# One step of the preparation reordered in a fused attention and MLP kernel, and one small sum moved to another PSUM bank

## The chip, the cores and the metric

The kernel runs on one core of a Trainium2 chip. A core has a matrix engine (TensorE, PE in the profile, with its weight loads as PEld), a vector engine (VectorE, DVE), a scalar engine (ScalarE, ACT), a general engine (GpSimd, POOL) and SyncE (SP), which issues most DMAs here. The metric is the device time of one execution in microseconds, as the median over several runs. Lower is better.

## What is computed

The input x has 2048 tokens of 640 numbers. A layer normalization gives xn, and two blocks read it side by side:

```
xn  = layernorm(x)
A   = attention(xn @ wqkv) @ wo        # 32 heads of 20, softmax over 2048 keys
B   = gelu(layernorm(xn) @ w1 + b1) @ w2 + b2    # 640 -> 1536 -> 640, per token
out = x + A + B
```

All inputs are float32. The kernel splits most numbers into a high and a low 16-bit part and multiplies in three passes (high x high, high x low, low x high), so that a product costs three matmuls.

## The kernel before

The kernel has two stages. The first is a preparation, about the first 183 us. It normalizes the tokens, turns them so that the feature axis lies on the partitions, and projects them to queries, keys and values. The second stage is a long loop over 16 pairs of heads, where the attention's scores and products alternate with pieces of the MLP. The change lies in the preparation alone.

**Chunks and steps.** The preparation takes the tokens in four chunks (c = 0 to 3) of 512. For each chunk it makes five products (tt = 0 to 4) of 30 matmuls, `qk(c, tt)` at L352, each giving 256 rows of the queries and keys. Right after a product is issued, a string of letters says which other work is issued then, letter by letter. Instructions run on each engine in the order in which they are issued, and SyncE's queue takes its DMAs in that order too. Nothing is reordered later by a planner: a manual schedule is in force, and waits are set by data alone. So the string is the order of work on every engine at once.

**The letters that the change touches** are those of chunk 0, product 4:

- `4`: `lengths(4)`, the squared lengths of four blocks, 16 small matmuls on TensorE (L397).
- `!`, `@`, `#`: `transp`, the transposes of the next chunk (chunk 1) on TensorE (L314), two feature blocks each for the first two and one for the third. `!` and `@` write to score buffers in PSUM, `#` to the one-bank pool `psM`.
- `t`: `transp_out`, which takes the oldest turned tile out of PSUM: ScalarE writes the high part (L321), VectorE the low part (L322). The third `t` also issues the store of the whole turned chunk to memory, `xscr`, on SyncE (L324). The main loop reads it much later.
- `o`: `qk_out`, which takes the product just made out of PSUM (ScalarE L367, VectorE L368) and issues two stores, `qkscr` (L373).
- `c`: `norm_c`, the last three small operations (L249 to L251) for the rows' factors `rall` of chunk 1. They are read at the end of the preparation.
- `q`: a load of one row block of w1, 768 KB (L545). `y`: a load of two row blocks of w2, 640 KB (L539). `x`: `load_x(2)`, four loads of chunk 2's tokens, 320 KB each (L197). All on SyncE.
- `S`: squares of the product's result on ScalarE (L384). `w`: the scale of the value weights (`scale_of`, L118 and L119 on) and their split (L476, L477). `z`: the next slice of the second layer's scale, a sum of squares over the rows of w2 that the latest `y` loads brought, on ScalarE (L530).

**Around it.** Chunk 1, product 0 issues `zos`: ScalarE squares the rows of w2 from the second `y` (L530), then `qk_out`, then a slice of w1's squares (L507). Chunk 1, product 1 issues, among others, `a` (`norm_a(2)`: the statistics of chunk 2's tokens on VectorE, L263 and L264), `b` (`norm_b(2)`, L278) and `i`, which with `j`, `k`, `l` is `turn`: ScalarE and VectorE split a tile into high and low parts (L333, L334), and SyncE issues a turning DMA (L335). Chunks 2 and 3 are turned by those DMAs, chunk 1 by TensorE.

**PSUM.** `psS` has three score buffers of two banks, `psO` one bank and `psM` one bank. A product, a transposed pair and most scale sums take the next free buffer of `psS`. `pow2(acc, tag)` at L109 to L126 turns sums of squares into a power of two: two matmuls with ones (L118) add over the partitions, and VectorE reduces and rounds (L119 on). The tag tells which weights: q, k, v, o, 1, 2 or b1. The first layer's scale, tag 1, is asked for in chunk 1, product 4, just ahead of chunk 2's first product. `psM` is what the MLP's products use in the main loop; in the preparation it also holds key lengths and the third transposed block.

Of the kernel before, what the change touches and what calls it, by code (L numbers as in the profile page):

```python
# [48 lines left out]
def mha_mlp_kernel(tc, x, wqkv, wo, w1, b1, w2, b2, out):  # L49
# [4 lines left out]
    with (  # L54
# [53 lines left out]
        def pow2(acc, tag, total=None):  # L108

            lo = keep.tile([P, 1], F32, name=f"lo_{tag}")  # L110
            hi = keep.tile([P, 1], F32, name=f"hi_{tag}")
            if total is None:
                if tag in "ko":
                    pt = psM.tile([P, 512], F32, tag="m", name="mxp")
                else:
                    pt = psS.tile([P, 2, 512], F32, tag="s", name="mxp")[:, 0, :]
                n = acc.shape[1]
                nc.tensor.matmul(pt[:, :n], ones_of[0], acc, start=True, stop=True)  # L118
                nc.vector.tensor_reduce(lo, pt[:, :n], AX.X, ALU.add)  # L119
                total = lo  # L120
            nc.vector.tensor_scalar(lo, total, 2.0**-100, 2.0**120, ALU.max, ALU.min)

            nc.vector.tensor_scalar(lo.bitcast(I32), lo.bitcast(I32), 0x7F000000, 1,
                                    ALU.bitwise_and, ALU.logical_shift_right)
            if tag == "q":

                scales[tag] = keep.tile([P, 1], F32, name=f"s_{tag}")
                nc.vector.tensor_scalar(hi.bitcast(I32), lo.bitcast(I32), 0x3F800000, None, ALU.bitwise_xor)
                nc.vector.tensor_scalar(scales[tag], hi, 2.0**76, None, ALU.mult)
                return lo, hi  # L130
            whole(lo, hi)
            return lo, hi

        def whole(lo, hi):
            nc.vector.tensor_scalar(lo, lo, 2.0**64, None, ALU.mult)
            exponents(lo, hi)
# [42 lines left out]
        with tc.tile_pool(name="pa", bufs=2) as pa, tc.tile_pool(name="pa1", bufs=1) as pa1, tc.manual_schedule():  # L179
# [103 lines left out]
            def norm_b2(c):  # L283
                mv, ve, r, r2 = rs[c]

                nc.vector.tensor_mul(ve, r, r)
                nc.vector.scalar_tensor_tensor(ve, ve, 2.0**-20, mv[:, :, 1], ALU.mult, ALU.mult)
                nc.vector.tensor_scalar(ve, ve, EPS, None, ALU.add)
                nc.gpsimd.tensor_tensor(r2, ve, nhalf, ALU.pow)

            def norm_c(c):
                mv, ve, r, r2 = rs.pop(c)
                newton(r2, ve, "b")
# [49 lines left out]
            def qk(c, tt, mid=None):  # L343
                ps = psS.tile([P, 2, 512], F32, tag="s", name="qkp")
                order = [(i, k) for i in range(2) for k in range(KD)]
                if c == 0 and tt < 2:

                    order = [(i, k) for k in range(KD) for i in range(2)]
                for i, k in order:
                    q, mm = divmod(2 * tt + i, KD)  # L350
                    for n, (a, b) in enumerate(PASS):
                        nc.tensor.matmul(ps[:, i, :], wv[:, k, q, a, mm * P : (mm + 1) * P],  # L352
                                         xnts[c][:, k, b, :], start=(k + n == 0), stop=(k == KD - 1 and n == 2))
                    if mid and (i, k) == (1, 2):
                        mid()
                return ps
# [98 lines left out]
            def sums(tag, ws):  # L455
                accs[tag] = squares(ws, junk)

            def scale_of(tag, total=None):
                pw[tag] = pow2(accs[tag], tag, total)
                if tag not in scales:  # L460
                    scales[tag] = keep.tile([P, 1], F32, name=f"s_{tag}")
                    nc.vector.tensor_scalar(scales[tag], pw[tag][1], 4096.0, None, ALU.mult)
                if tag == "k":
                    back(tag)
# [8 lines left out]
            def split_qkv(n, ks=range(KD), c0=0, c1=D):  # L473
                q = "qkv".index(n)
                for k in ks:
                    nc.scalar.activation(wv[:, k, q, 0, c0:c1], stage[n][:, k, c0:c1], AF.Copy, scale=scales[n])  # L476
                    nc.vector.scalar_tensor_tensor(wv[:, k, q, 1, c0:c1], stage[n][:, k, c0:c1], scales[n],  # L477
                                                   wv[:, k, q, 0, c0:c1], ALU.mult, ALU.subtract)
# [72 lines left out]
            def ask(n):  # L551
                for _ in range(n):
                    next(asked, None)
# [3 lines left out]
            def some(n):  # L557
                for _ in range(n):
                    next(slices, None)
# [60 lines left out]
            for c in range(4):  # L620
                nxt = c + 1 if c < 3 else None
                for tt in range(5):
                    if c == 0 and tt == 1:
                        norm_b2(0)
                        norm_c(0)

                        nc.scalar.activation(junk[:, :1], ones[:, :1], AF.Exp)
                        ps = qk(0, 1, lambda: scale_of("k"))
                        hl = qk_out(0, 0, first)
                        split_qkv("q", c0=4 * P)  # L630
                        split_qkv("k")
                    else:
                        ps = qk(c, tt)
                    if c == 0:
                        if tt == 0:
                            split_qkv("q", c0=2 * P, c1=4 * P)
                            sums("k", [stage["k"][:, 0:3], stage["k"][:, 3:]])
                            first = ps
                            continue
                        elif tt == 1:  # L640
                            qk_sq(0, 0, hl)
                            pts = []
                    for step in (('', 'qvo', 'ao', 'bo', '4q!y@c#otyxttSywz'), ('zos', 'qa6yqoPsbiqs', 'jkso', 'lcsV4o', 'sxoy'), ('ssoa6bzijP', 'yo', 'zs4ossc', 'klozV', 'uozs'), ('so', 'os6', 'oszs', 'ssosPsVfze4', 'o'))[c][tt]:
                        if step == "a":
                            norm_a(nxt)
                        elif step == "b":
                            norm_b(nxt)
                        elif step == "c":
                            norm_c(nxt)
                        elif step in "!@#":  # L650
                            transp(1, 2 * "!@#".index(step), pts)
                        elif step == "t":
                            transp_out(*pts.pop(0))
                        elif step in "46":
                            lengths(int(step))
                        elif step == "x":
                            load_x(c + 2)
                        elif step == "s":
                            some(1)
                        elif step == "q":  # L660
                            ask(1)
                        elif step == "z":
                            next(slices2, None)
                        elif step == "y":
                            next(asked2, None)
                        elif step == "v":
                            sums("v", [stage["v"][:, 0:3], stage["v"][:, 3:]])
                        elif step == "w":
                            scale_of("v")
                            split_qkv("v")  # L670
                        elif step == "u":
                            for s in range(2):
                                nc.sync.dma_start(vwscr[:, :, s], wv[:, :, 2, s, VC:])
                        elif step == "f":
                            factors_out()
                        elif step == "S":
                            qk_sq(0, 4, hl)
                        elif step == "o":
                            hl = qk_out(c, tt, ps)
                        elif step == "P":  # L680
                            vp = vproj(c - 1)
                        elif step == "V":
                            head_values(c - 1, vp)
                        elif step == "e":
                            early = [load_features(mc) for mc in range(2)]
                        else:
                            turn(nxt, "ijkl".index(step))
# [789 lines left out]
```

## Time and profile before

| | us |
|---|---|
| median of 3 runs | 1329.0 (1326.13 to 1329.7) |
| the profiled execution | 1328.16 |
| its span, first to last instruction | 1326.3 |
| TensorE busy | 1314.0 |
| ScalarE busy | 1116.3 |
| VectorE busy | 1065.3 |

The profile is of one execution. Its span is what the instructions cover, and the execution's own time is a little longer. A busy share is an average over the whole span: TensorE's 99% hides a few short waits in the preparation, and what a change there is worth is read from the order of time around it, from who waits for whom. An engine's idle time before an instruction stands in square brackets, with the one that ended it. That name is inferred from the semaphores: where an instruction waits for several, it is the one that came last by the profile, and it can be wrong. DMAs are seen as issues on SyncE's queue (their length is the time in the queue, not the transfer), as bytes moved per time, and through the waits that they end.

### The profile page before, as it was taken

What the parts mean: (1) busy time and instruction counts of PE and PEld (TensorE: products, weight loads), DVE (VectorE), ACT (ScalarE), POOL (GpSimd) and SP (SyncE); (2) the same over time, 40 slices, a digit from 0 to 9 for tenths busy, and PEclk for the clock granted to TensorE, in tenths of its full rate; (3) what the DMA queues carried; (4) which work ended last, traced back from release to release, by engine and by line L of the source; (5) the groups of instructions that cost most, each with busy time, mean ns of one, the idle gap of its engine ahead of it and who ended that gap; (6) DMA issues with size and microseconds to landing.
All of it is one profiled execution on the core that took longest, in us unless ns stands there. A gap on an engine that the chain in (4) does not pass through costs nothing.

```text
span 1326.3 us, 29078 instructions
## 1 busy us (share of the span) xinstructions
PE 1314.0 (99%) x11636; PEld 604.2 (46%) x11636; DVE 1065.3 (80%) x1450; ACT 1116.3 (84%) x1306; POOL 36.1 (3%) x85
## 2 busy tenths in 40 slices
PE   9999999999999999999999999999999999999998
PEld 6454564333344444444444444444444444443466
DVE  7667569898699887889988798987889898988642
ACT  7745369999999999999999999999999999989900
POOL 2000000000000000000000000000000000000000
PEclk9999999999999999999999999999999999999999
DMA  8697531121233321142312034222124332253266
GB/s 308 215 276 214 190 103 35 39 63 53 77 82 99 86 57 33 44 120 64 97 47 68 17 88 123 69 55 58 50 59 117 92 87 70 71 158 100 87 216 192
DMA packets 108166, 135.28 MB, mean 102 GB/s; under 512 B 24308, under 2 KB 74376, under 8 KB 107900
## 3 DMA queue, kind: packets, MB, share of 16 engines
q1 hardware_dynamic: 104588, 125.99, 31.9%
q0 software_dynamic: 2816, 6.90, 2.7%
q8 instruction: 92, 1.51, 0.5%
q10 hardware_dynamic: 624, 0.51, 0.1%
q14 instruction: 46, 0.38, 0.1%
HBM read 86.64 MB, written 43.74 MB: 98 GB/s over the span
## 4 chain that ended last, share of the span: by engine, by line
PE 72%; DVE 15%; ACT 5%; DMA 4%; issue 2%; SPq 1%; ACTq 0%; DVEq 0%; POOLq 0%
PE o L818 23%; PE s L786 15%; PE pu L1079 10%; PE py L1114 8%; DVE low L800 6%; PE qkp L352 6%; PE z L1264 5%; PE pz L1166 3%; ACT p L788 2%; PE vp L425 1%; DMA xb<-in_B_b_dram 1%; DVE w L1014 1%; DVE u L1012 1%; DVE u L1010 1%; DVE w L1016 1%
## 5 line engine op out<-in xcount | busy, mean ns | idle before, releaser
L788 ACT ACTIVATE p<-s 128x1024 f32<-128x1024 f32 x1024 | 968.7, 1057 | 56.2 <-PE s L786 53.9
L800 DVE TENSOR_TENSOR low<-p 128x1024 f16<-128x1024 f32 x512 | 605.7, 1219 | 72.8 <-ACT p L788 71.4
L818 PE MATMUL o<-p,vfull 128*32 128x512 bf16 (+1 forms) x4096 | 384.1, 493 | 0.0
L786 PE MATMUL s<-qs,ks 61*128 61x512 f16 x2048 | 303.5, 381 | 3.0 <-ACT p L788 2.1
L786 PEld LDWEIGHTS <-ks 61*128 61x128 f16 x2048 | 75.7, 94 | 234.8 <-issue 215.8
L1114 PE MATMUL py<-w2t,hT 128*128 128x320 f16 x1152 | 171.5, 300 | 0.9 <-DVE xb L1041 0.9
L1079 PE MATMUL pu<-xm,w1t 128*128 128x256 f16 x1440 | 171.4, 273 | 0.1
L1079 PEld LDWEIGHTS <-w1t 128*128 128x128 f16 x1440 | 134.3, 98 | 43.9 <-issue 29.3
L818 PEld LDWEIGHTS <-vfull 128*32 128x32 f16 x3072 | 61.1, 95 | 183.3 <-issue 182.7
L1114 PEld LDWEIGHTS <-hT 128*128 128x128 f16 x1152 | 105.6, 98 | 71.2 <-issue 33.9
L352 PE MATMUL qkp<-xnt,wv 128*128 128x512 f16 x600 | 131.4, 379 | 1.6 <-DVE lo L119 0.8
L818 PE MATMUL o<-low,vfull 128*32 128x512 f16 x1024 | 101.5, 378 | 0.1
L352 PEld LDWEIGHTS <-wv 128*128 128x128 f16 x600 | 58.0, 98 | 70.9 <-issue 1.7
L818 PEld LDWEIGHTS o<-p,vfull 128*32 128x32 f32 x2048 | 61.8, 108 | 58.3
L1264 PE MATMUL z<-w1t,ot 128*128 128x320 f16 x480 | 66.7, 299 | 0.0
L1010 DVE TENSOR_TENSOR u<-pu,r2f 128x512 f32<-128x512 f32 x48 | 33.1, 689 | 36.2 <-PE pu L1079 36.0
L1264 PEld LDWEIGHTS <-ot 128*128 128x128 f16 x480 | 46.3, 98 | 21.0 <-issue 3.3
L367 ACT ACTIVATE qkhl<-qkp,qks 128x1024 f16<-128x1024 f32 (+1 forms) x24 | 23.2, 965 | 37.2 <-PE qkp L352 15.3
L1221 DVE SCALAR_TENSOR_TENSOR acc<-z,sc,acc 128x320 f32<-128x320 f32 x32 | 17.6, 550 | 42.0 <-PE z L1264 41.7
L368 DVE SCALAR_TENSOR_TENSOR qkhl<-qkp,qks,qkhl 128x1024 f16<-128x1024 f32 (+1 forms) x24 | 26.5, 1105 | 26.1 <-ACT qkhl L367 26.0
L843 ACT ACTIVATE ev<-o 128x512 f32<-128x512 f32 x64 | 39.5, 617 | 3.0 <-PE o L818 2.8
L1104 POOL DMA_DIRECT2D xb<-in_B_b_dram x16 | 13.7, 857 | 953.7 <-DMA xb<-in_A_x_dram 352.4
(206 smaller groups left out, 735.2 us busy)
## 6 DMA issues: line engine op xcount, KB each, us to landing
qkscr<-qkhl SPq DMA_DIRECT2D x40, 256.0 KB
opart<-ev SPq DMA_DIRECT2D x124, 80.0 KB
ks<-qkscr SPq DMA_DIRECT2D x120, 80.0 KB
xm<-xscr SPq DMA_DIRECT2D x13, 640.0 KB
qs<-qkscr SPq DMA_DIRECT2D x192, 40.0 KB
oa<-opart SPq DMA_DIRECT2D x32, 240.0 KB
xt<-in_A_x_dram SPq DMA_DIRECT2D x16, 320.0 KB
xscr<-xnt SPq DMA_DIRECT2D x4, 1280.0 KB
```

Source lines behind the costliest of these rows:

```text
L352: nc.tensor.matmul(ps[:, i, :], wv[:, k, q, a, mm * P : (mm + 1) * P], xnts[c][:, k, b, :], start=(k + n == 0), stop=(k == KD - 1 and n == 2))
L368: nc.vector.scalar_tensor_tensor(hl[:, 1, i0:i1], ps[:, i0:i1], a, hl[:, 0, i0:i1], ALU.mult, ALU.subtract)
L786: nc.tensor.matmul(ps[:, a, :], ks[64 * a : 64 * a + 61, kb * P : (kb + 1) * P], qs[64 * a : 64 * a + 61, cc * 512 : (cc + 1) * 512], star ...
L788: nc.scalar.activation(pt, ps, AF.Exp, scale=QS)
L800: nc.vector.tensor_sub(low, pt, upper(pt))
L818: nc.tensor.matmul(pv.o[32 * q : 32 * q + 32, :], src[:, v0 - PAD * (1 - q % 2) :][:, :32], t, start=q not in pv.begun, stop=last, skip_gr ...
L843: nc.scalar.activation(evs[g, hf][:, cc], o, AF.Copy)
L1010: nc.vector.tensor_mul(u, ps, r2f[:, None, :].to_broadcast([P, 2, MC]))
L1079: nc.tensor.matmul(ps[:, i], w1v[:, k, (f + i) // 4, a, fo_ : fo_ + P], xnt[:, k, b, :], start=(n == 0), stop=(n == 3 * KD - 1))
L1114: nc.tensor.matmul(ps[:, :320], hTs[mc][:, f, a, j * P : (j + 1) * P], w2v[:, f, b, hf * 320 : (hf + 1) * 320], start=(n == 0), stop=(n == ...
L1166: nc.tensor.matmul(ps[:, : D - VC], feats[c][:, k, a, j * P : (j + 1) * P], hv[:, k, b, :], start=(n == 0), stop=(n == 3 * KD - 1))
L1264: nc.tensor.matmul(ps[:, :320], ot[:, k, a, j * P : (j + 1) * P], wov[:, k, b, h * 320 : (h + 1) * 320], start=(n == 0), stop=(n == 3 * KD ...
```

## The change

It has two parts. In the string of chunk 0, product 4 the three transposes now come ahead of the lengths, the factors `c` come after two turned tiles in place of before the third transpose, and with that the DMAs change places: the w1 load comes after the first w2 load, and the third turned tile, with its store, comes ahead of the second w2 load and of the four token loads. The set of letters is the same, and no other step's string differs. In `pow2`, tag 1 joins k and o: its sum is made in `psM` in place of a score buffer.

```diff
             if total is None:
-                if tag in "ko":
+                if tag in "ko1":
                     pt = psM.tile([P, 512], F32, tag="m", name="mxp")
                 else:
                     pt = psS.tile([P, 2, 512], F32, tag="s", name="mxp")[:, 0, :]
...
-                    for step in (('', 'qvo', 'ao', 'bo', '4q!y@c#otyxttSywz'), ('zos', 'qa6yqoPsbiqs', 'jkso', 'lcsV4o', 'sxoy'), ...
-                    for step in (('', 'qvo', 'ao', 'bo', '4q!y@c#otyxttSywz'), ('zos', 'qa6yqoPsbiqs', 'jkso', 'lcsV4o', 'sxoy'), ('ssoa6bzijP', 'yo', 'zs4ossc', 'klozV', 'uozs'), ('so', 'os6', 'oszs', 'ssosPsVfze4', 'o'))[c][tt]:
+                    for step in (('', 'qvo', 'ao', 'bo', '!y@#4qottctyxSywz'), ('zos', 'qa6yqoPsbiqs', 'jkso', 'lcsV4o', 'sxoy'), ('ssoa6bzijP', 'yo', 'zs4ossc', 'klozV', 'uozs'), ('so', 'os6', 'oszs', 'ssosPsVfze4', 'o'))[c][tt]:
```

## The prediction

> **What bounds the kernel now.** I read the page first, then the chain that ended last, in order of time, then the stretch from 47 to 92 us instruction by instruction, and last SyncE's issues with the bytes that the DMAs moved.
>
> ```profile
> span 1326.3 us, 29078 instructions
> PE 1314.0 (99%) x11636; PEld 604.2 (46%) x11636; DVE 1065.3 (80%) x1450; ACT 1116.3 (84%) x1306; POOL 36.1 (3%) x85
> PE 72%; DVE 15%; ACT 5%; DMA 4%; issue 2%; SPq 1%; ACTq 0%; DVEq 0%; POOLq 0%
> ```
>
> Over the whole span TensorE is the bound. The reordered step lies near 50 us, so the chain around it decides (start, length, what):
>
> ```profile
> 49.07 0.17 DVE bt L250
> ...
> 49.38 1.28 DVE qkhl L368
> 50.67 1.14 DVE xnt L322
> ...
> 51.85 13.11 PE qkp L352 x60
> 64.96 0.26 PE norms L397 x8
> ...
> 65.25 0.69 DVE sq L386
> 65.94 0.81 DVE st L263 x2
> ...
> 75.50 0.74 DVE row L334
> ...
> 76.28 2.53 SPq L335
> ```
>
> Up to 51.85 us VectorE sets the pace, then TensorE until 64.96. Then VectorE normalizes the third chunk (65.25 to 76.24, back to back), and from 76.28 SyncE issues the DMAs that turn it. TensorE meets that chunk at 90.48:
>
> ```profile
> SPq L338 <- DMA xnt<-row: 2.7, 1, 2.7
> 90.45 1.64 PEld L352 LDWEIGHTS <-wv 128*128 128x128 f16 x9 [0.89 <-issue]
> 90.46 0.56 SPq L338 DMA_DIRECT2D xscr<-xnt  x1
> 90.48 1.89 PE L352 MATMUL qkp<-xnt,wv 128*128 128x512 f16 x8 [0.83 <-DVE lo L119]
> 90.48:182.80 92.32, 92.31 (x649) 51.10 (x649) 56.85 (x134) 37.02 (x63) 5.91 (x9) 1.00 0.66 193
> ```
>
> The matmul's wait of 0.83 us is put down to the reduction at L119. But the weight load ahead of it started at 90.45, and SyncE's store at 90.46 ended a wait for the turned chunk itself, so I read all three as released by the last turning DMA. The last row (a window, TensorE's busy time first) shows TensorE without a gap from there to 182.80. So whatever moves the third chunk's turning moves everything behind it.
>
> **The change part by part.**
>
> *Transposes ahead of the lengths, factors later (TensorE and VectorE).*
>
> ```profile
> 47.43 0.41 PE L397 MATMUL norms<-sq,heads 128*32 128x128 bf16 x16
> 47.68 1.28 DVE L368 SCALAR_TENSOR_TENSOR qkhl<-qkp,qks,qkhl 128x1024 f16<-128x1024 f32 x1
> 49.02 1.53 PE L314 MATMUL pt<-ident,xt 128*128 128x128 f32 x12 [0.16 <-DVE qkhl L368]
> 50.59 2.94 DVE L322 TENSOR_TENSOR xnt<-pt,xnt 128x1024 f16<-128x1024 f32 x3
> 50.73 0.38 PE L118 MATMUL mxp<-acc,ones 128*128 128x2 f32 x2 [0.17 <-DVE qkhl L368]
> 51.85 13.11 PE L352 MATMUL qkp<-xnt,wv 128*128 128x512 f16 x60 [0.75 <-DVE xnt L322]
> ```
>
> The three small factor operations (L249 to L251) stand between the two L368 and hold the second one from 47.68 + 1.28 = 48.96, when the first has ended, to 49.38. Moved behind two turned tiles they let it start 0.4 us earlier, and the first L322 and TensorE's start at 51.85 follow: minus 0.4 us. The bounds are 0 and the whole wait of 0.75 us. The 16 lengths matmuls (0.41 us) now come after the transposes, which end at 49.02 + 1.53 = 50.55 because their second group still waits for the first L368. With the lengths and the two L118 matmuls (0.41 + 0.38) TensorE is ready at 51.34, just before 51.45, so they cost nothing; 0.1 us of cover is left. The third tile's L322 now follows the factors, but VectorE's total work there is unchanged, so it still ends at 50.59 + 2.94 = 53.53. The product of 51.85 takes the five blocks in order, three matmuls each, so it needs the fifth, which is the third tile, after 12 x 13.11 / 60 = 2.6 us, at 54.07: covered by 0.5 us. No instruction of POOL is moved.
>
> *SyncE's queue.* This is the part that I expect to cost. Each row: start, time in the queue.
>
> ```profile
> 49.42 0.46 SPq L545 DMA_DIRECT2D w1t<-in_B_w_dram  x1
> 49.93 0.44 SPq L539 DMA_DIRECT2D w2t<-in_B_w_dram  x1
> 50.47 1.24 SPq L373 DMA_DIRECT2D qkscr<-qkhl  x2
> 51.76 0.93 SPq L539 DMA_DIRECT2D w2t<-in_B_w_dram  x1
> 52.78 2.79 SPq L197 DMA_DIRECT2D xt<-in_A_x_dram  x4
> 56.92 0.54 SPq L324 DMA_DIRECT2D xscr<-xnt  x1
> w2t<-in_B_w_dram SPq DMA_DIRECT2D x5, 640.0 KB
> xscr<-xnt SPq DMA_DIRECT2D x2, 1280.0 KB
> 48.50:59.85 11.35, 10.27 (x56) 5.36 (x55) 9.87 (x19) 8.59 (x12) 0.32 (x1) 1.00 0.87 287
> 52.00:56.00 4.00, 4.00 (x20) 1.80 (x19) 2.93 (x9) 2.03 (x3) 0.00 (x0) 1.00 0.87 274
> 57.00:66.00 9.00, 9.00 (x71) 4.43 (x70) 4.54 (x7) 7.36 (x10) 0.00 (x0) 1.00 1.06 400
> ```
>
> Step q (a load of w1) goes behind the first y (a load of w2), an exchange within the queue worth nothing: both are used much later. But the third t issues the store of the turned chunk, xscr, 1280 KB, and it now stands ahead of the second y and of x's four loads. It can issue at about 53.6, when the third L322 ends. The queue is full: the windows' last column says 400 GB/s from 57 to 66 us. It also serves about in order: from 48.50 to 59.85 it moved 11.35 x 287 = 3.26 MB, and the issues up to and with the second y, with one store of 256 KB at 48.99, are 2.88 MB. So the second y's load lands later by the time of the store: 1.311 MB / 400 GB/s = 3.3 us. And ScalarE waits for just that load:
>
> ```profile
> 59.85 1.27 ACT L530 ACTIVATE junk<-w2t 128x1280 bf16<-128x1280 f32 x1 [0.32 <-DMA w2t<-in_B_w_dram]
> 61.12 1.09 ACT L367 ACTIVATE qkhl<-qkp,qks 128x1024 f16<-128x1024 f32 x1
> 62.25 1.28 DVE L368 SCALAR_TENSOR_TENSOR qkhl<-qkp,qks,qkhl 128x1024 f16<-128x1024 f32 x1 [2.75 <-ACT qkhl L367]
> 65.25 0.69 DVE L386 TENSOR_TENSOR sq<-qkhl 128x1024 bf16<-128x1024 f16 x1 [1.71 <-PE norms L397]
> 65.86 0.88 DVE L263 BATCH_NORM_STATS2 st<-xt 128x6 f32<-128x320 f32 x2
> ```
>
> Queued behind L530 on ScalarE are L367, and through it VectorE's L368, L386 and the third chunk's statistics L263. With 3.3 us more, L530 starts at 63.15, L367 at 64.42, L368 runs from 65.55 to 66.83, and L386 starts at about 66.8 in place of 65.25: 1.71 us of the delay are swallowed by the wait that L386 has today, 1.55 us are left. The four loads of x shift by the same 3.3 us; today they are in the queue just behind the second y, 1.31 MB, so they have landed by 59.85 + 3.3 = 63.2 and will by about 66.5. The statistics would start at 67.4 and read the four tiles 1 us apart: covered.
>
> From L386 on the chain passes the delay through, since VectorE is back to back to 76.24, and the turning DMAs follow it: plus 1.55 us at 90.48, and so at the end. The 0.4 us gained at 51.85 are not taken off, since L386 is then no longer held by TensorE. Bounds of this part: if the load isn't held by the store, minus 0.4 (rival below); at the 274 GB/s of 52 to 56 us, store and load take 4.8 + 2.4 us in place of 1.6 for the load alone, 5.6 us more, less 1.7: plus 3.8. I take 1.55, since the store will fall into the stretch of the 400 GB/s row.
>
> [...]
>
> *The first layer's scale in the MLP's bank.* The sum's two matmuls leave the pool of three score buffers for the one-bank pool of the MLP, idle then; the next product takes another buffer. By the reading of the three rows at 90.45 to 90.48 the product waits for the turned chunk, not for a buffer: 0. Bounds: 0 and minus 0.83, the whole wait.
>
> **Sum.** 0 (covered) + 1.55 + 0 = plus 1.55 us on the profiled execution: its own time is 1328.16, 1.86 more than its span, so 1329.7. It lies 0.84 below the median of the three runs (1329.0); on that scale I predict 1330.5.
>
> **The rivals.**
> 1. *The load isn't held.* It lands within the 1.71 us of slack: then the 0.4 us at 51.85 counts, 1328.6. For it: loads read memory and the store writes it. Against it: the byte count. It decides if the load lands before 61.5.
> 2. *The buffer was the wait.* If the 0.83 us at 90.48 really belongs to L119, and the load isn't held, both gains count: 1329.0 - 0.4 - 0.83 = 1327.8. For it: the releaser in the row. Against it: the weight load and the store at 90.45.
> 3. *The store drains slowly* (the other side: slower by over 4 us). At 274 GB/s it costs plus 3.8, at 268 plus 4.0, and 1333.0 or more is reached. For it: the rate of 52 to 56. Against it: 400 GB/s from 57 on. It decides if the load lands at 65.6 or later, 4.0 + 1.7 after today's 59.85.
>
> **How the numbers follow.** A measurement of this kernel tells about 0.3% (4 us) from no change; the three runs spread over 3.6 us. Likeliest 0.50; rival 1 0.18; rival 2 0.07; rival 3 0.25. The likeliest's own range is 1328.5 to 1333, by the spread of runs. With rivals 1 and 2 at the low end less half that spread, and rival 3 up to a load 3 us later still, the range is 1326.3 to 1336. Slower by over 0.3%: rival 3 nearly whole and a tenth of the likeliest, 0.30. Faster by over 0.3%: rivals 1 and 2 in a low draw, 0.06. Within: 0.64.
>
> **What would show it.** Right: the second L322 group starts at about 50.2, TensorE's first product of the second chunk at 51.45; xscr is issued near 53.6 ahead of w2t; L530's second wait ends near 63.2 with a DMA named; L386 near 66.8 with ScalarE or nothing named in place of PE; the third chunk's first product at about 92. Wrong: L530's wait still ends near 60, or the third chunk starts at 90 or before. The prediction also fails if later stages between 92 and 183 us have slack that I don't see, or if the attention loop behind them doesn't keep its length.

## The result and the profile after

| | before | after |
|---|---|---|
| median | 1328.01 us (12 runs) | 1331.09 us (12 runs) |
| lowest to highest | 1326.13 to 1329.70 | 1329.74 to 1335.24 |
| the profiled execution | 1328.16 | 1332.08 |
| its span | 1326.3 | 1330.1 |

The changed kernel is slower: the ratio is 1.0026, with a 95% interval of 1.0017 to 1.0035, so 3.5 us (2.3 to 4.6). The median of before is over more runs than the three shown ahead of the prediction, and lies 1 us below theirs. One execution of bank_back, a kernel below, ran at a granted clock of 0.654 and took 1865.91 us; it is left out of that kernel's numbers.

The page of the kernel after, first its span and the busy times:

```profile
span 1330.1 us, 29079 instructions
...
PE 1314.6 (99%) x11636; PEld 603.9 (45%) x11636; DVE 1065.0 (80%) x1450; ACT 1115.9 (84%) x1306; POOL 36.3 (3%) x85
```

No engine is busy for more than 0.6 us longer than before. The time is in waits. The timeline of the kernel after, around the reordered step (start, length, instruction, and in brackets the idle time before it with what ended it):

```profile
47.90 2.48 DVE L368 SCALAR_TENSOR_TENSOR qkhl<-qkp,qks,qkhl 128x1024 f16<-128x1024 f32 x2
...
50.29 2.36 DVE L322 TENSOR_TENSOR xnt<-pt,xnt 128x1024 f16<-128x1024 f32 x2
...
51.56 13.11 PE L352 MATMUL qkp<-xnt,wv 128*128 128x512 f16 x60
...
53.74 0.54 SPq L324 DMA_DIRECT2D xscr<-xnt  x1
...
54.33 1.13 SPq L539 DMA_DIRECT2D w2t<-in_B_w_dram  x1
...
55.55 5.00 SPq L197 DMA_DIRECT2D xt<-in_A_x_dram  x4
...
64.17 1.27 ACT L530 ACTIVATE junk<-w2t 128x1280 bf16<-128x1280 f32 x1 [4.45 <-DMA w2t<-in_B_w_dram]
...
65.44 1.10 ACT L367 ACTIVATE qkhl<-qkp,qks 128x1024 f16<-128x1024 f32 x1
...
66.57 1.28 DVE L368 SCALAR_TENSOR_TENSOR qkhl<-qkp,qks,qkhl 128x1024 f16<-128x1024 f32 x1 [6.88 <-ACT qkhl L367]
67.77 0.68 DVE L386 TENSOR_TENSOR sq<-qkhl 128x1024 bf16<-128x1024 f16 x1
```

Both L368 now run back to back, the first two L322 start at 50.29, and the second chunk's product at 51.56 has no wait. Then the new queue order shows: the store at 53.74, the second load of w2 behind it, and ScalarE at L530 waiting 4.45 us for that load (0.32 before). L367, L368 and L386 come late in a row. L386 has no wait left, where it had 1.71 us for TensorE.

Further on, the turning DMAs and the third chunk, on the SyncE queue of the kernel after:

```profile
78.80 1.48 SPq L335 DMA_TRANSPOSE xnt<-row  x1
...
81.14 6.94 SPq L335 DMA_TRANSPOSE xnt<-row  x2
...
93.97 0.56 SPq L338 DMA_DIRECT2D xscr<-xnt  x1
```

From the first turning DMA to the store that waits for the turned chunk it takes 15.17 us, against 90.46 - 76.28 = 14.18 before.

TensorE in the kernel after, and then its windows (columns: stretch, its length, busy time and instructions of PE, PEld, DVE, ACT and POOL, granted clock, DMA share, GB/s):

```profile
94.11 8.32 PE L352 MATMUL qkp<-xnt,wv 128*128 128x512 f16 x30 [3.49 <-DVE sq L386]
```

```profile
52.00:56.00 4.00, 4.00 (x20) 1.85 (x19) 2.86 (x12) 2.07 (x3) 0.00 (x0) 1.00 0.96 309
...
48.50:64.10 15.60, 14.80 (x90) 7.51 (x90) 10.05 (x19) 8.69 (x12) 0.54 (x1) 1.00 0.91 299
...
94.00:98.00 4.00, 3.90 (x11) 1.45 (x12) 3.43 (x15) 0.72 (x1) 0.00 (x0) 0.57 0.72 240
98.00:102.00 4.00, 4.00 (x20) 1.79 (x19) 0.00 (x0) 0.00 (x0) 0.00 (x0) 1.00 1.00 290
```

TensorE now waits 3.49 us for the third chunk, where it waited 0.83. The first product behind that wait takes 8.32 us, and the same product before took 6.63. The windows tell why: from 94 to 98 us the granted clock is 0.57, and then 1.00 again. TensorE has by then already waited 1.19 us ahead of the product before that one (at 83.85, for VectorE's L368); in the kernel before it did not wait there.

Executions differ in their start-up, so the table counts from one event in each kernel: the start of VectorE's L368 for product 3 of chunk 0 (47.68 before, 47.90 after). The attention loop starts with ScalarE's first L788. Each number is from one profiled execution.

| kernel | second L530 starts (its wait) | L386 starts | third chunk's product starts | its length | attention loop starts | loop's length |
|---|---|---|---|---|---|---|
| before | 12.17 (0.32) | 17.56 | 42.80 | 6.63 | 135.86 | 1142.72 |
| after | 16.27 (4.45) | 19.87 | 46.20 | 8.32 | 140.95 | 1141.23 |
| store_back | 11.98 (0.17) | 17.05 | 41.88 | 6.63 | 134.94 | 1141.36 |
| store_early | 16.17 (4.32) | 19.76 | 46.03 | 6.63 | 139.09 | 1141.40 |
| bank_only | 12.16 (0.31) | 17.56 | 43.49 | 6.63 | 136.55 | 1143.45 |
| square_late | 15.84 (1.56) | 17.05 | 43.20 | 6.63 | 136.26 | 1143.09 |
| load_ahead | 13.02 (0.03) | 18.24 | 43.09 | 6.63 | 136.16 | 1141.04 |
| store_twice | 19.55 (6.56) | 23.16 | 49.20 | 9.43 | 145.05 | 1143.62 |
| bank_back | 16.22 (4.41) | 19.82 | 45.19 | 8.32 | 139.94 | 1143.23 |
| clock_kept | 16.02 (4.21) | 19.62 | 45.85 | 6.63 | 138.91 | 1145.27 |
| fill_six | 16.14 (4.33) | 19.75 | 45.18 | 6.63 | 138.24 | 1142.43 |
| lengths_early | 11.95 (0.13) | 15.55 | 41.32 | 6.63 | 134.38 | 1143.30 |
| after_again | 16.00 (4.18) | 19.60 | 46.06 | 8.32 | 140.81 | 1141.72 |

From before to after: 0.22 us by the event itself, 2.31 at L386, 1.09 more until the third chunk's product, 1.69 in that product, and the loop, which in this execution is 1.49 shorter. That is 3.8 us, the difference of the spans.

### The profile page after: what moved, and what is told of

Its sections match the earlier page's. It is cut to its first block, busy times and chain, and to the rows that moved or that the text cites. A ratio compares the mean times of both kernels' runs of the same rounds, so it can differ in the third digit from the quotient of the medians.

```text
span 1330.1 us, 29079 instructions
## 1 busy us (share of the span) xinstructions
PE 1314.6 (99%) x11636; PEld 603.9 (45%) x11636; DVE 1065.0 (80%) x1450; ACT 1115.9 (84%) x1306; POOL 36.3 (3%) x85
## 4 chain that ended last, share of the span: by engine, by line
PE 82%; DVE 8%; ACT 5%; DMA 3%; issue 2%; SPq 0%; ACTq 0%; DVEq 0%
PE o L818 27%; PE s L786 17%; PE pu L1079 11%; PE py L1114 11%; PE qkp L352 5%; PE z L1264 5%; PE pz L1166 3%; DVE low L800 3%; ACT p L788 3%; PE vp L425 1%; DMA w2t<-in_B_w_dram 1%; DMA xb<-in_B_b_dram 1%; PE vp L446 1%; DVE qkhl L368 1%; ACT wv L476 1%
## 5 line engine op out<-in xcount | busy, mean ns | idle before, releaser
L788 ACT ACTIVATE p<-s 128x1024 f32<-128x1024 f32 x1024 | 968.7, 1055 | 55.2 <-PE s L786 53.2
L367 ACT ACTIVATE qkhl<-qkp,qks 128x1024 f16<-128x1024 f32 (+1 forms) x24 | 23.2, 965 | 35.4 <-PE qkp L352 19.7
L368 DVE SCALAR_TENSOR_TENSOR qkhl<-qkp,qks,qkhl 128x1024 f16<-128x1024 f32 (+1 forms) x24 | 26.4, 1105 | 30.4 <-ACT qkhl L367 30.4
```

Source lines behind the costliest of these rows:

```text
L368: nc.vector.scalar_tensor_tensor(hl[:, 1, i0:i1], ps[:, i0:i1], a, hl[:, 0, i0:i1], ALU.mult, ALU.subtract)
L788: nc.scalar.activation(pt, ps, AF.Exp, scale=QS)
```

## The experiments

**store_back.** The changed kernel with the store back behind the loads; transposes first, factors later and the bank are kept.

```diff
-'!y@#4qottctyxSywz'
+'!y@#4qottcyxtSywz'
```

> The changed kernel, with the store of the turned chunk put back behind the second w2 load and the four token loads (the third turned tile is taken out one step later; TensorE's, VectorE's and ScalarE's order stay as changed). My theory, the store in SyncE's queue: ScalarE's second L530 waits under 0.6 us again in place of 4.45, the third chunk's first product starts at 89.5 to 90.5 in place of 94.11, and the time is 0 to 1 us below the kernel before (1327 to 1328). Rival, the order on TensorE and VectorE costs: it stays 3 us above the kernel before (1331).

Measured: 1328.75 us against 1328.55 for before; ratio 1.0001 (0.9991 to 1.0010). L530's wait in its timeline:

```profile
58.83 0.54 SPq L324 DMA_DIRECT2D xscr<-xnt  x1
...
61.83 1.27 ACT L530 ACTIVATE junk<-w2t 128x1280 bf16<-128x1280 f32 x1 [0.17 <-DMA w2t<-in_B_w_dram]
...
66.89 0.69 DVE L386 TENSOR_TENSOR sq<-qkhl 128x1024 bf16<-128x1024 f16 x1 [1.39 <-PE norms L397]
```

With the store behind the loads the whole loss is gone. The earlier transposes bring L386 0.5 us forward, but no gain in time that can be told.

**store_early.** The kernel before with the store alone moved ahead.

```diff
-'4q!y@c#otyxttSywz'
+'4q!y@c#otttyxSywz'
```

> The kernel before, with one thing changed: the third turned tile, and with it the store, stands ahead of the second w2 load and the four token loads; lengths, transposes, factors and the bank stay as before. My theory: L530 waits 4 to 4.7 us, the third chunk's first product starts at 93.5 to 94.5, and the time is 3.0 to 3.6 us above the kernel before. Rivals, the order of transposes and factors, or the bank: no difference to the kernel before, within 0.5 us.

Measured: 1332.21 us against 1328.55, ratio 1.0029 (1.0019 to 1.0040). L530 waits 4.32 us and L386 starts at 19.76 from the event. The store's place alone gives the whole loss.

**bank_only.** The kernel before with the first layer's scale in the MLP's bank.

```diff
-                if tag in "ko":
+                if tag in "ko1":
```

> The kernel before, with the first layer's scale summed in the MLP's bank and nothing else. My theory: no difference to the kernel before (within 0.5 us), since the wait at 90.48 is for the turned chunk. Rival, the buffer was the wait: 0.8 us faster. Rival, the bank is part of the loss: slower by 1 us or more.

Measured: 1328.62 us, ratio 1.0003 (0.9993 to 1.0014): nothing. The wait ahead of the third chunk did not go (1.52 us in this execution), so it wasn't for a buffer.

**square_late.** The changed kernel with ScalarE's square of w2 (`z`) moved behind the two other letters of its step, so that L367 no longer stands behind it.

```diff
-('zos', 'qa6yqoPsbiqs', ...
+('osz', 'qa6yqoPsbiqs', ...
```

> The changed kernel, with the squares of the late w2 rows (L530) issued on ScalarE behind the next product's way out (L367) and a slice of w1's squares, in place of ahead of them; the store stays ahead of the loads. My theory, the loss goes through ScalarE's order: the load still lands near 64, but L367 starts at about 59.8, the third chunk's first product at 90 to 91, and the time is 0.5 us below to 0.7 above the kernel before. Rival, the loss goes through the late token loads or through the slower queue as such: it stays 2 us or more above.

Measured: 1328.10 us, ratio 0.9995 (0.9986 to 1.0004). Its timeline:

```profile
61.01 1.09 ACT L367 ACTIVATE qkhl<-qkp,qks 128x1024 f16<-128x1024 f32 x1
...
65.13 1.27 ACT L530 ACTIVATE junk<-w2t 128x1280 bf16<-128x1280 f32 x1 [1.56 <-DMA w2t<-in_B_w_dram]
...
66.34 0.69 DVE L386 TENSOR_TENSOR sq<-qkhl 128x1024 bf16<-128x1024 f16 x1 [2.92 <-PE norms L397]
```

The load is as late as in the changed kernel (L530 starts 15.84 from the event), but only the squares wait for it. L386 is back at 17.05 and the loss is gone. So a late load does no harm by itself: what stands behind its reader on ScalarE does.

**load_ahead.** The changed kernel with the second load of w2 ahead of the store, and the four token loads still behind it.

```diff
-'!y@#4qottctyxSywz'
+'!y@#4qottcytxSywz'
```

> The changed kernel, with the second w2 load alone put back ahead of the store; the four token loads stay behind it. My theory, the loss goes through the w2 load that ScalarE waits for, not through the token loads: L530 waits under 1 us, the third chunk's first product starts 42 to 43.3 us after the L368 of the first chunk's fourth product (before: 42.8, changed: 46.2), and the time is within 0.8 us of the kernel before. Rival, the late token loads cost: the statistics L263 wait for a DMA, and the time is 2 us or more above.

Measured: 1328.45 us against 1328.36, ratio 0.9996 (0.9987 to 1.0005). The token loads behind the store cost nothing, as the prediction had it; the one load of w2 is the whole path.

**store_twice.** The changed kernel with a second store of the turned chunk, to memory that nothing reads: more work, the result untouched.

```diff
+        xscr2 = dram.tile([P, KD, 2, 512], F16, name="xscr2")
...
+                    nc.sync.dma_start(xscr2, xnts[c])
```

> The changed kernel, with the store of the turned chunk issued twice, the second time to a place that nothing reads (the result is not touched). My theory, the loss follows the bytes ahead of the load: L530 waits 7.5 to 8.5 us in place of 4.45, the third chunk's first product starts 3 to 4 us later than in the changed kernel, and the time is 2.5 to 4 us above the changed kernel (about 1334.5). Rival, it is the exchange of order as such and not the bytes: like the changed kernel, 1331 to 1332.

Measured: 1335.95 us, ratio 1.0053 (1.0041 to 1.0065), so 0.0027 or 3.6 us more than the changed kernel's ratio. Its timeline (its line numbers are one or two higher):

```profile
56.68 0.54 SPq L325 DMA_DIRECT2D xscr<-xnt  x1
...
69.22 1.27 ACT L532 ACTIVATE junk<-w2t 128x1280 bf16<-128x1280 f32 x1 [6.56 <-DMA w2t<-in_B_w_dram]
```

The squares wait less than the 7.5 to 8.5 us expected, and start 3.28 us later from the event than in the changed kernel, which is 1.311 MB at 400 GB/s. The first store is issued 1.2 us later in this execution (7.0 us behind the event against 5.8), but the queue is still busy with the DMAs ahead of it: by the packets in the traces the first bytes of that store land at 59.10, 9.4 us behind the event, against 57.67 or 9.8 us in the changed kernel. From there to the squares it takes 10.1 us in place of 6.5, 3.6 us more. So the delay follows the bytes ahead of the load, at 3.3 to 3.6 us for 1.311 MB.

**clock_kept.** The changed kernel with 14 added products of ones in the wait for the third chunk, so that TensorE isn't idle; the result is untouched.

```diff
-'sxoy'
+'Wsxoy'
...
+                        elif step == "W":
+                            fill_ = psM.tile([P, 512], F32, tag="m", name="fill")
+                            for _ in range(14):
+                                nc.tensor.matmul(fill_[:, :P], ones, ones, start=True, stop=True)
```

> The changed kernel, with 14 products of ones put on TensorE in the wait ahead of the third chunk (to the idle bank, read by nobody). Theory: the wait of 3.5 us lets the granted clock fall, so that the first product behind it takes 8.3 us in place of 6.6. With the wait filled that product takes 6.6 us, the granted clock of that stretch is near 1.00 in place of 0.79, and the time is 1.0 to 1.7 us below the changed kernel. Rival, the slow matmuls have another cause (code loading, DMA traffic): the product stays at 8 us or more and the time at 1331 to 1332.

Measured: 1334.27 us over 6 runs, ratio 1.0040 (1.0028 to 1.0053), a miss. The mechanism works where it was aimed: the product takes 6.63 us again, at a granted clock of 1.00 from 94 to 98 us, and the loop starts 2.04 us earlier than in the changed kernel. The added products were too many, though: SyncE issues the store that waits for the turned chunk at 93.14, and TensorE starts the product only at 94.03, where 0.13 us lie between the two in fill_six below. But the loop of this execution is 4.04 us longer than the changed kernel's. Part of that can be named. Late in the loop VectorE waits for a load of the bias that GpSimd issues, and TensorE waits for VectorE; first clock_kept, then the kernel after:

```profile
1194.94 0.55 DVE L1045 SCALAR_TENSOR_TENSOR xb<-py,sc,xb 128x320 f32<-128x320 f32 x1 [4.16 <-DMA xb<-in_B_b_dram]
...
1195.54 2.88 PE L1118 MATMUL py<-w2t,hT 128*128 128x320 f16 x20 [2.72 <-DVE xb L1045]
```

```profile
1193.44 0.55 DVE L1041 SCALAR_TENSOR_TENSOR xb<-py,sc,xb 128x320 f32<-128x320 f32 x1 [1.97 <-DMA xb<-in_B_b_dram]
...
1194.05 2.88 PE L1114 MATMUL py<-w2t,hT 128*128 128x320 f16 x20 [0.54 <-DVE xb L1041]
```

That is 2.2 of the 4.0 us. The same wait is 0.95 us in the kernel before and 1.01 in lengths_early, so it varies from one profiled execution to another.

**after_again, bank_back, fill_six.** Three kernels side by side on one chip, to tell the clock from the added matmuls: the changed kernel once more, the changed kernel with the bank undone, and clock_kept with 6 added products in place of 14.

```diff
-                if tag in "ko1":
+                if tag in "ko":
```

```diff
-                            for _ in range(14):
+                            for _ in range(6):
```

> The changed kernel once more, as the base for the two beside it on one chip. All theories: ratio to the kernel before 1.0026 give or take 0.001, the third chunk's first product 46.2 us after the fifth value product's end step (start of VectorE's L368 for product 3 of chunk 0), 8.3 us long instead of 6.6.

> The changed kernel with the first layer's scale back in a score buffer; the order of the step stays. The sum's two matmuls then split TensorE's wait for the third chunk into some 0.7 and 2.4 us, as in store_early. If the split keeps the granted clock up and the time follows the end of the preparation, the product is back at 6.63 us, the attention loop starts some 1.7 us earlier than in the changed kernel, and the time is 1.7 us below it (ratio to the kernel before 1.0013). If the loop gives such a gain back, the product is shorter and the time is that of the changed kernel, ratio 1.0026. If only the transposes' order mattered for the clock, the product stays at 8.3 us.

> The changed kernel with 6 instead of 14 added products of ones in front of the wait for the third chunk (extra work, nothing of the result changes): 1.4 us of added matmuls in a wait of 3.5 us, so that 2.1 us stay idle. All theories: the product takes 6.63 us, as with 14. If the added matmuls themselves are what made the time longer (1.004 with 14), the ratio is between, near 1.0032 less the clock's 0.0013; if clock_kept was slow by the draw of its six runs, the ratio is that of bank_back, 1.0013; if the loop gives back what the clock wins, it is 1.0026.

Measured: after_again 1331.68 us, ratio 1.0024 (1.0013 to 1.0035), again a wait of 3.62 us and a product of 8.32. bank_back 1333.07, ratio 1.0033 (1.0020 to 1.0046). fill_six 1332.88, ratio 1.0043 (1.0028 to 1.0057), above all three of the ratios expected. The kernel before took 1328.00 beside them. The windows of bank_back, and then of fill_six:

```profile
94.00:98.00 4.00, 4.00 (x12) 1.50 (x11) 3.26 (x13) 0.72 (x1) 0.00 (x0) 0.57 0.91 306
...
265.00:270.00 5.00, 4.97 (x31) 1.35 (x31) 4.57 (x10) 3.72 (x5) 0.00 (x0) 0.66 0.18 50
```

```profile
94.00:98.00 4.00, 4.00 (x20) 1.86 (x19) 2.91 (x11) 0.72 (x1) 0.00 (x0) 1.00 1.02 340
```

In bank_back TensorE's wait is split into 0.32 and 1.94 us around the sum's two matmuls, and the clock fell all the same; in store_early it is split into 0.71 and 2.44 and the clock stayed at 1.00. So the split is not what decides; the last section takes this up. With 6 added products the clock stayed too, and fill_six's loop starts 2.7 us earlier than the changed kernel's. Yet its median is no better: its executions lie between 1330.12 us at a granted clock of 1.000 and 1336.68 at 0.995. Its three executions at 0.999 or 1.000 took 1330.12 to 1331.98 us, like after_again's four at that clock (1329.67 to 1332.63), so its high median goes with the three at 0.995 to 0.998. In clock_kept it isn't the clock: five of its six executions ran at 0.999 or 1.000, and took 1331.05 to 1335.79. Why they are slow stays open, beyond the added products that outlasted the wait and the load of the bias. What the runs do say is that keeping the clock up at the third chunk did not make the kernel faster.

**lengths_early.** store_back, and the next six lengths (`6`, 24 small matmuls) one product earlier, at chunk 1, product 0: L386 then need not wait behind that product for TensorE.

```diff
-'!y@#4qottctyxSywz'), ('zos', 'qa6yqoPsbiqs', ...
+'!y@#4qottcyxtSywz'), ('z6os', 'qayqoPsbiqs', ...
```

> The changed kernel with the store put back behind the loads, and besides the six lengths of the second chunk's second product issued one product earlier, so that VectorE's L386 no longer waits for TensorE. Theory: L386 and the third chunk's normalization start 1.5 us earlier, TensorE's wait ahead of the third chunk (0.4 to 0.8 us) goes, and the time is 0.5 to 1.3 us below the kernel before. Rival, that wait is set by the turning DMAs' own length: no gain, within 0.4 us.

Measured: 1326.98 us (1325.10 to 1327.72), ratio 0.9985 (0.9976 to 0.9994): faster than both kernels. Its timeline:

```profile
58.15 0.52 PE L397 MATMUL norms<-sq,heads 128*32 128x128 bf16 x24
...
59.88 1.27 ACT L530 ACTIVATE junk<-w2t 128x1280 bf16<-128x1280 f32 x1
...
63.48 0.68 DVE L386 TENSOR_TENSOR sq<-qkhl 128x1024 bf16<-128x1024 f16 x1
...
89.25 6.63 PE L352 MATMUL qkp<-xnt,wv 128*128 128x512 f16 x30
```

L386 starts 2.0 us earlier than in the kernel before, without a wait, and TensorE meets the third chunk without a wait. In this execution the loop starts 1.48 us earlier from the event; the ratio says 2.0 us (0.8 to 3.2), where 0.5 to 1.3 were expected. Against store_back, which lacks only the moved lengths, the profiled loop starts 0.56 us earlier, so not all of the gain is accounted for.

## Why the prediction was right or wrong

The time predicted was 1330.5, and 1331.09 was measured, within the range and within 0.3% as its likeliest case said. The change itself was forecast as +1.55 us, and it is +3.5 (2.3 to 4.6): the mechanism was right and the sum too small. That the time came within 0.6 us is in part luck: the sum was about 2 us short, and the three runs that it was set on lay 1 us above the later median.

*Transposes ahead, factors later.* Right in kind: from the event the second chunk's product starts at 3.66 in place of 4.17, so 0.5 us earlier where 0.4 was forecast. As the prediction said, it gives nothing while L386 waits for ScalarE. store_back, which keeps it, isn't faster either, by what can be measured.

*SyncE's queue.* The path was right link by link: the store at 53.74 (forecast 53.6), L530 waiting for the load of w2, L367 and L368 behind it, the slack at L386 gone, the token loads covered. store_early brings the whole loss with the store alone, and store_back, load_ahead and square_late each cut the path at another link and lose it. The mis-sized term is the store's time: 3.3 us at 400 GB/s, measured 4.1 (16.27 - 12.17). To the second load's landing the queue moved 15.60 x 299 = 4.66 MB after and 11.35 x 287 = 3.26 MB before, so the 1.40 MB more took 15.60 - 11.35 = 4.25 us: 330 GB/s, between the two rates that the prediction had. The store itself did not run in the slow stretch of 52 to 56 us: it was issued at 53.74, but by the packets in the trace its 1280 pieces of 1 KB landed only from 57.67 to 61.72 us. That is 4.05 us for 1.311 MB, with 65 packets of the loads behind it, 0.17 MB, among them. The prediction gave the store the full 400 GB/s of a later stretch; it got 1.311 MB / 4.05 us = 324. The slack took 4.10 - 2.31 = 1.79 us (forecast 1.71), which leaves 2.31 at L386 in place of 1.55. The load of w2 did not overtake the store: the store's last packet landed at 61.72, and the load released ScalarE at 64.17. Those 65 packets of later loads did land ahead of the store's last one, but the load as a whole did not.

*"From L386 on the chain passes the delay through."* This step failed as an equality. The turning DMAs start 2.3 us late, as L386 does, but they end 3.3 us late: the stretch takes 15.17 us in place of 14.18. It is 15.21 in store_early and 13.66 in store_back, but also 14.64 in square_late and 14.93 in lengths_early, where no such delay stands ahead, and 14.22, 14.32 and 14.27 in bank_back, clock_kept and fill_six, where it does. So the stretch differs by up to 1.6 us between profiled executions, whether L386 is late or not. Why it was long in this one stays open. The third chunk's product started at 94.11, where about 92 was forecast.

*A term that was missing.* TensorE's wait grew to 3.49 us, and behind it the granted clock fell, 1.69 us more in that product. The prediction took the product's length as given. It is not a safe part of the loss, though: store_early has its full loss with the clock up.

*The bank.* Right: 0, by bank_only. The reading that the wait of 0.83 us belongs to the turned chunk and not to the L119 named in the row holds; in the kernel after the same wait is put down to L386, in after_again to L119, and it is neither. In square_late the product starts at 92.49, before L386 ends (92.33 + 0.68 = 93.01), and in the kernel after at 94.11, before L119 ends (94.00 + 0.16 = 94.16). But in every profile in which TensorE waits right ahead of it, it starts 0.02 to 0.17 us behind SyncE's L338, which waits for the turned chunk.

*The loop keeps its length.* Not within 1 us: between 1141.0 and 1145.3 us over twelve kernels whose loops are the same. The sum over one execution can't be better than that.

*The rivals.* That the load isn't held (1) and that the buffer was the wait (2) are out by L530's 4.45 us and by bank_only. The slow drain (3) is out by its own sign, a landing at 65.6 or later: the load released ScalarE at 64.17. It had a point in that the store was slower than the 400 GB/s taken, but not the 274 that it feared.

## What to carry to other kernels

In a queue that serves about in order, as SyncE's did here (0.17 MB of later loads landed ahead of the store's last packet, the load of w2 as a whole behind it), a store moved ahead of a load costs the load the store's bytes over the queue's rate at that time (here 3.3 to 4.1 us for 1.311 MB), and the reader's place on its own engine decides whether anything waits: give the load's reader nothing urgent behind it, or keep stores behind the loads. A slack found in the trace (here 1.71 us at L386) can be moved on purpose too: putting TensorE's lengths one product earlier removed that wait and gave the one version that was faster. Where a change makes TensorE wait (2.26 to 3.62 us in the four profiles here in which the clock fell), look at the granted clock behind the wait as well as at the wait, but don't count on a gain in the whole from keeping it up: here there was none.

## What the runs showed of the hardware

- The granted clock fell at the waits for the third chunk of 3.49 us (after), 3.62 (after_again), 3.21 (store_twice) and 0.32 + 1.94 (bank_back), and stayed at 1.00 with 0.71 + 2.44 (store_early), 1.74 (square_late) and 0.87 (fill_six). The product behind it took 1.7 us more (2.8 in store_twice, where the clock was 0.96 from 94 to 98 us and 0.50 from 98 to 102). The length of the wait alone doesn't decide: 2.26 us in bank_back cost the clock, and 3.15 us in store_early did not. In the kernel after, windows of 94.00:94.50, 94.50:97.50 and 97.50:98.00 have a clock of 0.85, 0.50 and 0.74, so it was at half from 94.35 to 97.76, for 3.41 us. How busy TensorE was over a stretch of that length, up to the start of the product, doesn't decide either; here TensorE in bank_back and in store_early:

```profile
91.02 0.39 PE L118 MATMUL mxp<-acc,ones 128*128 128x5 f32 x2 [0.32 <-ACT vfull L614]
93.34 8.32 PE L352 MATMUL qkp<-xnt,wv 128*128 128x512 f16 x30 [1.94 <-DVE qkhl L368]
```

```profile
91.34 0.39 PE L118 MATMUL mxp<-acc,ones 128*128 128x5 f32 x2 [0.71 <-ACT vfull L614]
94.17 2.10 PE L352 MATMUL qkp<-xnt,wv 128*128 128x512 f16 x9 [2.44 <-DVE qkhl L368]
```

  In the last 3.41 us ahead of the product TensorE was busy for 3.41 - 0.32 - 1.94 = 1.15 us in bank_back, and there the clock fell; in store_early it was busy for the 0.39 us of the sum alone, and the clock stayed. The other profiles lie on both sides: it fell where that stretch held no work (after, after_again) or 0.20 us (store_twice), and stayed where it held 1.67 (square_late). What decides it, these runs don't show.
- The clock also fell in the loop of some executions, at about the same place: near 265 us in bank_back (0.66 above), and near 260 in lengths_early, whose windows show it here:

```profile
257.00:262.00 5.00, 3.74 (x24) 1.17 (x28) 4.76 (x15) 4.95 (x6) 0.00 (x0) 0.76 0.58 168
262.00:267.00 5.00, 5.00 (x31) 1.63 (x23) 4.63 (x6) 2.35 (x3) 0.00 (x0) 0.90 0.00 0
```

  In the kernel after that place ran at 1.00, and in clock_kept too, where TensorE was busy for 3.75 us from 262 to 267, against 3.74 in the first of the rows above; so there, too, busy time alone doesn't decide. Nor did the wait of 2.72 us near 1195 us in clock_kept cost the clock: over that whole execution it is 1.000, and 3.41 us at half would make it 0.999. Together with the load of the bias near 1190 us, where TensorE's wait ran from 0.33 us (load_ahead) to 2.72 (clock_kept), such draws go some way to explain why executions of one kernel differ by some microseconds, and why a loop start that is 2 us earlier need not show in the median.
